# Another order for the first weight pairs of a fused attention and MLP kernel: a table of decode stages in place of whole steps

## The chip, the cores and the metric

The kernel runs on one core of one Trainium2 chip. The metric is the time of one execution on the device, in microseconds (us). The core's engines are named as in the profile: PE is TensorE's matmul (PEld its weight load), DVE is VectorE, ACT is ScalarE, POOL is GpSimd, and SP is SyncE, from whose queue nearly all transfers of this kernel are issued. Each engine runs its own instructions in the order in which they were put there and waits for the others by semaphores.

## The reference, cut to what matters

```python
def reference(q, k, v, n_sink, window, moe_w_in, moe_w_out, moe2_w_in, moe2_w_out):
    x = attention(q, k, v)      # 8 heads of 64, 2 x 768 tokens; a key is seen if it is one of the
                                # first 4 (sinks) or within 128 back
    h = x @ moe_w_in            # 1536 x 512 @ 512 x 2048
    y = (h - tanh(h)) @ moe_w_out
    h = y @ moe2_w_in
    return (h * clip(h + 3, 0, 6) / 6) @ moe2_w_out
```

All four weight matrices come as float64, 32 MB together. The rest is float32.

## The kernel before

**Tokens and groups.** The 1536 tokens are worked through in three chunks of 512. A chunk passes two MLPs, called phase 0 and phase 1. In a phase a hidden layer of 2048 is 16 blocks: h0 to h15 (x times a block of `w_in`, tile `ps_h`) and y0 to y15 (the gated block times a block of `w_out`, added up in four tiles `ps_y`). They run in the order h0, h1, h2, y0, h3, y1, h4, y2 and so on, with y14 and y15 last. One such group is 12 matmuls of 128x512: 4 blocks, three each, since every operand is split into a high and a low part (`mm3`, L178 to L180). Between an h and its y stands the gate: `th` on ACT (L230 in phase 0, L236 in phase 1), its difference or product on DVE (L232, L238), `gh` on ACT (L233, L239), and `gl` on DVE (L234, L240). After y15 the sums are cast to `yh` on ACT (L246, four of them), and phase 1 reads these.

**Weights.** Two groups share a pair of weights, 1 MB of float64. There are 32 pairs, and they are decoded on the chip while chunk 0 runs. The stages of a pair are `w_load` (a transfer on SP into one of 4 raw buffers), `w_scale` (ACT, `dec`, L110), `w_exponent` (DVE, L121), `w_sign` (ACT twice: the low word `r`, L130, and the high word, L132), `w_round` (DVE, L138), `w_keep` (a transfer on SP that stores the decoded pair in DRAM for chunks 1 and 2) and `w_split` (`wh` on ACT, L154, or on POOL for odd pairs from 5 on; `wl` on DVE, L155). There are 4 buffers for `dec`, 2 for `r`, 4 each for `wh` and `wl`. `w_step(p, half)` runs the stages of several pairs at staggered distances: the load of pair p+6, the split of p+1, the low and high word of p+3, and so on.

**Attention.** Chunk 0's attention is 8 heads in pieces (80 in all); its stages are the loads, the casts of k and q (L324, L326), scores on PE (L494), softmax (`sc`, L498 to L503 and L347), transposes of the sink part (`turn_sink`, L525, cast to `pskT` by ACT L529) and of the rest (`turn_p`, L539, copied to `p` by ACT L543), the product with v (`mix`, L588, reading `pskT`, `px` and `vs`), and the cast to the MLP's input (`xh`, L374; `xl` on DVE, L375). Heads 6 and 7 make the last of the four blocks of `xh`, so h0 can run on three blocks before attention has ended. The attention of chunks 1 and 2 is spread over the MLP of the chunk ahead.

**Who sets the order.** `startup` writes attention's pieces of chunk 0 with the first 12 halves of `w_step` among the last 18 of them; `rest` writes the MLP's steps, each with a `w_step`. All of it stands in a block with `schedule_with_timeline_sim=True`: a scheduler decides at build time in what order each engine gets the instructions. `keep_in_program_order` pins an instruction to its place among the others that are pinned.

Of the kernel before, what the change touches and what calls it, by code (L numbers as in the profile page):

```python
# [12 lines left out]
U32 = mybir.dt.uint32  # L13
ACTF = mybir.ActivationFunctionType
# [33 lines left out]
class Mlp:  # L48
# [74 lines left out]
    def w_sign(self, p):  # L123


        if p >= PAIRS:
            return
        raw = self.raw.pop(p)
        r = self.rr[p] = self.r_p.tile([128, 1024], I32, tag="r", name="r")
        self.nc.scalar.activation(out=r, in_=raw[:, :, 0].bitcast(U32), func=ACTF.Copy, scale=2.0 ** -29)  # L130
        upper = r.bitcast(F16).rearrange("p (n two) -> p n two", two=2)[:, :, 1]
        self.nc.scalar.activation(out=upper, in_=raw[:, :, 1].bitcast(F32), func=ACTF.Copy, scale=2.0 ** -100)  # L132

# [137 lines left out]
class Attention:  # L271
# [60 lines left out]
    def split_v(self, it):  # L332
        nc = self.nc
        s = self.st[it]
        s["vs"] = self.v_p.tile([128, len(s["kb"]), 2, 64], F32R, tag="vs", name="vs")
        vh = s["vs"][:, :, 0, :]
        nc.scalar.copy(out=vh, in_=s["vr"])
        nc.gpsimd.tensor_sub(out=s["vs"][:, :, 1, :], in0=s["vr"], in1=vh.bitcast(F32))

    def norm(self, s):  # L340
# [438 lines left out]
def banded(mlp, at):  # L779

    tc = mlp.tc
    with tc.block(schedule_with_timeline_sim=True):
        startup(mlp, at)
        at.wide = False
        rest(mlp, at)


def startup(mlp, at):
    at.sinks()
    first = [p for t in at.ticks(0) for p in t]  # L790
    warm = [(p, h) for p in range(-6, 0) for h in range(2)]
    for n, p in enumerate(first):
        p[0](*p[1:])
        left = len(first) - 1 - n
        while warm and left < 1.5 * len(warm):
            mlp.w_step(*warm.pop(0))


def rest(mlp, at):
# [82 lines left out]
```

## Time and profile before

| | |
|---|---|
| time, median of 3 runs | 682.88 us (680.9 to 683.8) |
| the profiled execution | 682.02 us |
| its span, first to last instruction | 680.3 us |
| PE busy | 635.3 us (93%) |
| DVE busy | 451.8 us (66%) |
| ACT busy | 433.4 us (64%) |
| POOL busy | 154.8 us (23%) |

The profile is of one execution, so sums made from it stand against its own 682.02 us, of which 1.7 us lie outside the span. That execution is 0.86 us under the median of the three runs. The shares are averages over the whole span, while the change touches only its beginning.

### The profile page before, as it was taken

The numbers are of one execution on the slowest core, as the hardware profiler recorded it, in microseconds if no ns is written. First come the engines' busy times: TensorE is split into PE (matmuls) and PEld (weight loads), VectorE is DVE, ScalarE is ACT, GpSimd is POOL, SyncE is SP. The second block draws the span as 40 slices with busy tenths as digits, with TensorE's granted clock in tenths as the row PEclk, the third lists the DMA queues.
The fourth block names the chain that finished last, engine by engine and source line by source line (L and its number), as shares of the span: only waits on it lengthen the run. The fifth ranks groups of instructions, "written<-read, shape, count | busy, mean of one in ns | idle before, by whom it ended". The sixth has DMA issues, their size and how long they took to land.

```text
span 680.3 us, 8590 instructions
## 1 busy us (share of the span) xinstructions
PE 635.3 (93%) x2952; PEld 509.3 (75%) x2952; DVE 451.8 (66%) x824; ACT 433.4 (64%) x742; POOL 154.8 (23%) x198
## 2 busy tenths in 40 slices
PE   1887799995999999999999999999999999999995
PEld 1654688874778778888888788888888888888884
DVE  5996789898799987454665686765454444455431
ACT  3899999999899965444555666655444444354421
POOL 1453011253265654200003344432100000000000
PEclk9997899998899999999999999999999999999998
DMA  5389999987678642233332433122133223221001
GB/s 165 106 275 356 351 377 307 337 303 253 253 239 287 245 168 73 89 123 124 115 120 83 153 112 111 63 87 100 63 124 124 86 101 104 83 69 55 1 0 66
DMA packets 26427, 106.31 MB, mean 156 GB/s; under 512 B 6152, under 2 KB 9224, under 8 KB 18184
## 3 DMA queue, kind: packets, MB, share of 16 engines
q1 hardware_dynamic: 26304, 105.67, 44.8%
q8 instruction: 25, 0.41, 0.2%
q14 instruction: 26, 0.21, 0.1%
q10 hardware_dynamic: 72, 0.02, 0.0%
HBM read 85.76 MB, written 19.92 MB: 155 GB/s over the span
## 4 chain that ended last, share of the span: by engine, by line
PE 66%; ACT 15%; DVE 10%; issue 4%; DMA 3%; POOL 0%; SPq 0%; DVEq 0%; ACTq 0%
PE ps_h L178 10%; PE ps_y L179 10%; PE ps_h L179 10%; PE ps_h L180 10%; PE ps_y L180 10%; PE ps_y L178 10%; ACT r L130 3%; PE ps_a L588 3%; ACT r L132 3%; ACT dec L110 3%; DVE dec L138 2%; DMA raw<-in_w_dram 1%; ACT sc L503 1%; PE ps_a L494 1%; ACT wh L154 1%
## 5 line engine op out<-in xcount | busy, mean ns | idle before, releaser
L179 PE MATMUL ps_y<-gl,wh 128*128 128x512 f32 x384 | 152.2, 396 | 0.5 <-DVE gl L234 0.3
L180 PE MATMUL ps_y<-gh,wl 128*128 128x512 f32 x384 | 151.0, 393 | 0.0
L178 PE MATMUL ps_y<-gh,wh 128*128 128x512 f32 x384 | 133.0, 397 | 7.3 <-ACT gh L233 7.3
L155 DVE TENSOR_TENSOR wl<-raw,wh 128x1024 fp32r<-128x1024 f32 x64 | 79.0, 1235 | 48.4 <-ACT wh L154 46.1
L154 ACT CAST wh<-raw 128x1024 fp32r<-128x1024 f32 x64 | 67.3, 1052 | 48.9 <-PE ps_y L179 36.9
L178 PEld LDWEIGHTS ps_y<-gh,wh 128*128 128x128 f32 x384 | 71.2, 189 | 21.3 <-ACT gh L233 7.5
L179 PEld LDWEIGHTS ps_y<-gl,wh 128*128 128x128 f32 x384 | 72.7, 189 | 17.1 <-DVE gl L234 1.4
L180 PEld LDWEIGHTS ps_y<-gh,wl 128*128 128x128 f32 x384 | 72.8, 189 | 14.9
L178 PE MATMUL ps_h<-xh,wh 128*128 128x512 f32 x192 | 77.0, 403 | 3.6 <-DVE th L232 3.6
L178 PE MATMUL ps_h<-yh,wh 128*128 128x512 f32 x192 | 76.4, 401 | 2.6 <-DVE th L238 2.4
L179 PE MATMUL ps_h<-xl,wh 128*128 128x512 f32 x192 | 76.7, 400 | 0.0
L180 PE MATMUL ps_h<-xh,wl 128*128 128x512 f32 x192 | 76.1, 398 | 0.0
L179 PE MATMUL ps_h<-yl,wh 128*128 128x512 f32 x192 | 76.0, 396 | 0.0
L180 PE MATMUL ps_h<-yh,wl 128*128 128x512 f32 x192 | 76.0, 396 | 0.0
L236 ACT ACTIVATE th<-ps_h,three 128x512 f32<-128x512 f32 x48 | 32.9, 686 | 53.0 <-PE ps_h L180 52.8
L230 ACT ACTIVATE th<-ps_h 128x512 f32<-128x512 f32 x48 | 28.6, 615 | 54.3 <-PE ps_h L180 44.7
L238 DVE SCALAR_TENSOR_TENSOR th<-th,ps_h 128x512 f32<-128x512 f32 x48 | 32.8, 684 | 40.8 <-ACT th L236 40.6
L232 DVE TENSOR_TENSOR th<-ps_h,th 128x512 f32<-128x512 f32 x48 | 32.6, 688 | 30.8 <-ACT th L230 30.6
L503 ACT ACTIVATE sc<-sc,mn 128x132 f32<-128x132 f32 x96 | 38.9, 406 | 14.9 <-DVE mn L499 14.4
L138 DVE CUSTOM_DVE_ANT_0 dec<-dec,r 128x2048 uint16<-128x2048 uint16 x32 | 41.7, 1302 | 9.1 <-ACT r L132 8.9
L178 PEld LDWEIGHTS ps_h<-xh,wh 128*128 128x128 f32 x192 | 36.8, 191 | 12.3 <-DVE th L232 4.0
L234 DVE TENSOR_TENSOR gl<-th,gh 128x512 fp32r<-128x512 f32 x48 | 34.5, 725 | 16.7 <-ACT gh L233 16.4
(105 smaller groups left out, 1150.4 us busy)
## 6 DMA issues: line engine op xcount, KB each, us to landing
raw<-in_w_dram SPq DMA_DIRECT2D x32, 1024.0 KB
raw<-keep SPq DMA_DIRECT2D x32, 1024.0 KB
keep<-dec SPq DMA_DIRECT2D x32, 512.0 KB
raw<-in_qkv_dram SPq DMA_DIRECT2D x8, 810.0 KB
raw<-in_qkv_dram SPq DMA_DIRECT2D x8, 486.0 KB
raw<-in_qkv_dram SPq DMA_DIRECT2D x6, 520.0 KB
out_dram<-ob SPq DMA_DIRECT2D x12, 256.0 KB
raw<-in_qkv_dram SPq DMA_DIRECT2D x8, 324.0 KB
```

The costliest lines, as they stand in the source:

```text
L138: self.nc.vector.tensor_tensor(out=t, in0=t, in1=self.rr.pop(p), op=ALU.add)
L154: nc.scalar.copy(out=wh, in_=src)
L155: nc.vector.tensor_sub(out=wl, in0=src, in1=wh.bitcast(F32))
L178: mm(out=ps, lhsT=wh, rhs=ah, start=first, stop=False)
L179: mm(out=ps, lhsT=wh, rhs=al, start=False, stop=False)
L180: mm(out=ps, lhsT=wl, rhs=ah, start=False, stop=last)
L230: nc.scalar.activation(out=th, in_=ps, func=ACTF.Tanh)
L232: nc.vector.tensor_sub(out=u, in0=ps, in1=th)
L234: self.late.append(lambda: nc.vector.tensor_sub(out=gl, in0=u, in1=gh.bitcast(F32)))
L236: nc.scalar.activation(out=th, in_=ps, func=ACTF.Relu, bias=self.three)
L238: nc.vector.scalar_tensor_tensor(out=u, in0=th, scalar=6.0, in1=ps, op0=ALU.min, op1=ALU.mult)
L503: nc.scalar.activation(out=s["sc"][:, i, :], in_=s["sc"][:, i, :], func=ACTF.Exp, scale=-1.0, bias=s["mn"][:, i:i + 1], accum_out=s["sm"][ ...
```

## The change

The 12 halves of `w_step` in `startup` are replaced by a table. Each row gives a number of attention pieces still to come, a stage and a pair; the stage is written when so many are left. Altogether the same stages of the same pairs are written ahead of `rest` as before. Two pins are added: the low-word pass (L130) of pairs 0 to 3, and the cast of v (L337) of chunk 1's heads 0 to 2.

```diff
@@ w_sign
-        self.nc.scalar.activation(out=r, in_=raw[:, :, 0].bitcast(U32), func=ACTF.Copy, scale=2.0 ** -29)
+        ins = self.nc.scalar.activation(out=r, in_=raw[:, :, 0].bitcast(U32), func=ACTF.Copy, scale=2.0 ** -29)
+        if p < 4:
+            self.tc.keep_in_program_order(ins)
@@ split_v
-        nc.scalar.copy(out=vh, in_=s["vr"])
+        ins = nc.scalar.copy(out=vh, in_=s["vr"])
+        if it[0] == 1 and it[1] < 3:
+            self.tc.keep_in_program_order(ins)
@@ startup
+WARM = (
+    (52, "load", 0), (48, "load", 1), (44, "load", 2), (40, "load", 3),
+    (36, "scale", 0), (33, "exponent", 0), (31, "sign", 0), (27, "round", 0),
...
+    (0, "exponent", 3), (0, "scale", 4),
+)
...
-    warm = [(p, h) for p in range(-6, 0) for h in range(2)]
+    warm = list(WARM)
     for n, p in enumerate(first):
         p[0](*p[1:])
-        left = len(first) - 1 - n
-        while warm and left < 1.5 * len(warm):
-            mlp.w_step(*warm.pop(0))
+        while warm and len(first) - 1 - n <= warm[0][0]:
+            _, stage, pair = warm.pop(0)
+            getattr(mlp, f"w_{stage}")(pair)
```

The line numbers of the changed kernel lie 2 higher from L132 on and 4 higher from L338 on (L134 is the high word, L156 `wh`, L180 to L182 the three matmuls, L232 `th`, L235 `gh`, L248 `yh`, L378 `xh`, L529 the sink's transpose, L533 `pskT`, L547 `p`).

**Place one, the end of attention, ACT.** Before, the last two casts `xh` stand among decode passes of several pairs (raw64_662 is pair 2, raw64_752 pair 5; 719 is pair 4, wh_787 and wh_845 are those of pairs 1 and 2):

```order
L374 CAST xh_131<-ps_a_736 64x512
L337 CAST vs_1249<-raw_1046 128x5x64
L529 CAST pskT_750<-ps_a_745 8x512
L110 ACTIVATE dec_774<-raw64_719 128x1024
L154 CAST wh_787<-dec_671 128x1024
L130 ACTIVATE r_818<-raw64_685 128x1024
L154 CAST wh_845<-dec_700 128x1024
L130 ACTIVATE r_872<-raw64_719 128x1024
L132 ACTIVATE r_818<-raw64_685 128x1024
L374 CAST xh_131<-ps_a_776 64x512
```

Now, from the cast `xh` of head 6 to the first gate (raw64_420 is pair 2, raw64_454 pair 3; the last cast `xh` is the one of head 7):

```order
L378 CAST xh_131<-ps_a_737 64x512
L339 CAST vs_1249<-raw_1046 128x5x64
L547 COPY p_758<-ps_a_753 128x512
L156 CAST wh_787<-dec_590 128x1024
L533 CAST pskT_751<-ps_a_746 8x512
L378 CAST xh_131<-ps_a_763 64x512
L110 ACTIVATE dec_774<-raw64_420 128x1024
L130 ACTIVATE r_777<-raw64_420 128x1024
L232 ACTIVATE th_806<-ps_h_793 128x512
L130 ACTIVATE r_818<-raw64_454 128x1024
L232 ACTIVATE th_838<-ps_h_823 128x512
```

Between the last two casts `xh` six decode passes stood and one stands now; pair 2 begins only behind attention. Counted over ACT's whole order, nine decode passes that stood ahead of the last cast `xh` stand behind it now: three `dec`, three low words, two high words and one `wh`.

**Place one, PE.** The transpose of head 7's sink part (now L529, ahead of `pskT`) stood in front of the MLP's first matmul before; now it stands behind 16 of them, and its `mix` behind 11 more. The rows are those around the transpose (ps_h_823 is h1, ps_h_851 is h2):

```order
L180 MATMUL ps_h_823<-xh_131,wh_608 128x512
L529 MATMUL ps_a_746<-ident_r_188,psk_734 8x128 x4
L181 MATMUL ps_h_823<-xl_132,wh_608 128x512
L182 MATMUL ps_h_823<-xh_131,wl_609 128x512
L180 MATMUL ps_h_851<-xh_131,wh_787 128x512
```

**Place two, the end of phase 0, ACT.** Before, the rows from `th` of h15 (th_1626) on (raw64_1663 and raw64_1762 belong to the same two pairs as dec_1808 and dec_1898):

```order
L230 ACTIVATE th_1626<-ps_h_1613 128x512
L326 ACTIVATE qh_1875<-raw_1671 128x512
L324 CAST k_1877<-raw_1671 128x660
L474 CAST vsk_1660<-vkr_1494 8x2x64
L132 ACTIVATE r_2080<-raw64_1762 128x1024
L110 ACTIVATE dec_1808<-raw64_1663 128x1024
L503 ACTIVATE sc_1570,sm_1572<-sc_1570,mn_1571 128x132
L337 CAST vs_1657<-raw_1491 128x5x64
L360 COPY ready1_70<-ps_a_1677 64x512
L503 ACTIVATE sc_1570,sm_1572<-sc_1570,mn_1571 128x132
L110 ACTIVATE dec_1898<-raw64_1762 128x1024
L529 CAST pskT_1747<-ps_a_1742 8x512
```

The next row was gh_1627, the gate of h15. Now:

```order
L232 ACTIVATE th_1626<-ps_h_1613 128x512
L134 ACTIVATE r_1805<-raw64_1537 128x1024
L130 ACTIVATE r_1895<-raw64_1605 128x1024
L235 CAST gh_1559<-th_1558 128x512
L328 ACTIVATE qh_1875<-raw_1671 128x512
L326 CAST k_1877<-raw_1671 128x660
L507 ACTIVATE sc_1570,sm_1572<-sc_1570,mn_1571 128x132
L235 CAST gh_1627<-th_1626 128x512
```

Behind the last gate, up to `yh`, stand rows that stood ahead of it. Ahead of the last `gh` of phase 0 ACT now has two `dec`, two low words, three high words, one `wh` and five small casts fewer. The four casts `yh` stood together; now a high word stands between the second and the third and a low word between the third and the fourth.

**Place three, SP.** Before, chunk 0's loads (raw_475 and raw_545 are q, k and v of heads 6 and 7; vkr is v at the sinks) came first, then the first pair (raw64_606):

```order
L459 DMA vkr_1278<-in_vs_dram 8x64 x2
L459 DMA vkr_1494<-in_vs_dram 8x64 x2
L267 DMA raw_405<-in_qkv_dram 128x4x260
L459 DMA vkr_1674<-in_vs_dram 8x64 x2
L267 DMA raw_475<-in_qkv_dram 128x4x260
L267 DMA raw_545<-in_qkv_dram 128x4x260
L94 DMA raw64_606<-in_w64_dram 128x2048
```

Now the four first pairs (raw64_363 to raw64_454) stand among them:

```order
L94 DMA raw64_363<-in_w64_dram 128x2048
L94 DMA raw64_392<-in_w64_dram 128x2048
L463 DMA vkr_1278<-in_vs_dram 8x64 x2
L463 DMA vkr_1494<-in_vs_dram 8x64 x2
L269 DMA raw_409<-in_qkv_dram 128x4x260
L94 DMA raw64_420<-in_w64_dram 128x2048
L94 DMA raw64_454<-in_w64_dram 128x2048
L269 DMA raw_485<-in_qkv_dram 128x4x260
```

So the first two pairs are ahead of the small loads `vkr` and of head 5's load, and the next two ahead of head 6's.

## Rows read from the trace of the kernel before

**Rows 1.** The page: the chain that ended last, by engine.

```profile
PE 66%; ACT 15%; DVE 10%; issue 4%; DMA 3%; POOL 0%; SPq 0%; DVEq 0%; ACTq 0%
```

**Rows 2.** Windows: stretch, length, busy us by engine (instructions), granted clock, DMA share, GB/s.

```profile
17.00:51.00 34.00, 29.22 (x166) 20.31 (x166) 31.63 (x121) 30.69 (x96) 16.59 (x29) 1.00 0.60 190
...
45.00:157.00 112.00, 103.41 (x457) 80.17 (x455) 96.12 (x151) 111.90 (x157) 29.95 (x30) 0.95 0.92 330
...
180.00:240.00 60.00, 59.25 (x302) 47.92 (x300) 57.48 (x101) 56.58 (x99) 31.64 (x32) 1.00 0.72 252
240.00:260.00 20.00, 18.30 (x96) 15.00 (x95) 17.30 (x34) 13.39 (x29) 13.11 (x16) 1.00 0.46 163
260.00:600.00 340.00, 339.26 (x1578) 275.64 (x1577) 196.01 (x328) 172.99 (x302) 55.87 (x78) 1.00 0.29 99
```

**Rows 3.** The wait of PE at the first gate: total, times, longest.

```profile
PE ps_h L178 <- DVE th L232: 3.6, 1, 3.6
```

**Rows 4.** Timeline of ACT at attention's end: start, duration, what.

```profile
58.69 0.57 ACT L543 COPY p<-ps_a 128x512 f32<-128x512 f32 x1
...
61.42 1.13 ACT L110 ACTIVATE dec<-raw 128x1024 f32<-128x1024 f32 x1
62.46 1.37 ACT L132 ACTIVATE r<-raw 128x1024 f16<-128x1024 f32 x1
63.70 0.56 ACT L374 CAST xh<-ps_a 64x512 fp32r<-64x512 f32 x1
...
66.04 1.03 ACT L154 CAST wh<-dec 128x1024 fp32r<-128x1024 f32 x1
66.97 1.15 ACT L130 ACTIVATE r<-raw 128x1024 int32<-128x1024 uint32 x1
68.03 1.03 ACT L154 CAST wh<-dec 128x1024 fp32r<-128x1024 f32 x1
...
71.39 0.58 ACT L374 CAST xh<-ps_a 64x512 fp32r<-64x512 f32 x1
...
81.74 1.17 ACT L233 CAST gh<-th 128x512 fp32r<-128x512 f32 x2
```

**Rows 5.** Timeline of PE at attention's end.

```profile
61.14 0.73 PE L178 MATMUL ps_h<-xh,wh 128*128 128x512 f32 x1
...
65.86 0.67 PE L588 MATMUL ps_a<-pskT,yh 8*64 8x512 f32 x2
...
68.12 0.50 PE L178 MATMUL ps_h<-xh,wh 128*128 128x512 f32 x1
68.45 0.39 PE L179 MATMUL ps_h<-xl,wh 128*128 128x512 f32 x1
68.68 0.40 PE L180 MATMUL ps_h<-xh,wl 128*128 128x512 f32 x1
...
80.11 0.63 PE L180 MATMUL ps_h<-xh,wl 128*128 128x512 f32 x1
80.54 0.63 PE L178 MATMUL ps_h<-xh,wh 128*128 128x512 f32 x1
```

**Rows 6.** Timeline of ACT at the end of phase 0.

```profile
168.50 0.61 ACT L233 CAST gh<-th 128x512 fp32r<-128x512 f32 x1
...
174.00 1.98 ACT L246 CAST yh<-ps_y 128x512 fp32r<-128x512 f32 x4
...
180.69 0.69 ACT L236 ACTIVATE th<-ps_h,three 128x512 f32<-128x512 f32 x1 [0.49 <-PE ps_h L180]
```

**Rows 7.** Timeline of PE: y15 (in brackets the idle time ahead of it).

```profile
169.16 2.08 PE L178 MATMUL ps_y<-gh,wh 128*128 128x512 f32 x4 [7.31 <-ACT gh L233]
```

**Rows 8.** Timeline of ACT, then of PE, at phase 1's first gate.

```profile
184.35 0.62 ACT L239 ACTIVATE gh<-th 128x512 fp32r<-128x512 f32 x1
...
186.36 1.14 PE L178 MATMUL ps_y<-gh,wh 128*128 128x512 f32 x4
```

**Rows 9.** The chain of waits, 30 to 40 us: start, length, what.

```profile
32.41 5.58 DMA raw<-in_w_dram
```

More of the change, by code (lines that the diff above doesn't have):

```diff
@@ L785, in banded @@
         rest(mlp, at)
+WARM = (
+    (52, "load", 0), (48, "load", 1), (44, "load", 2), (40, "load", 3),
+    (36, "scale", 0), (33, "exponent", 0), (31, "sign", 0), (27, "round", 0),
+    (24, "load", 4), (22, "scale", 1), (21, "keep", 0), (20, "split", 0), (18, "exponent", 1),
+    (13, "sign", 1), (8, "round", 1), (7, "keep", 1),
+    (0, "load", 5), (0, "scale", 2), (0, "exponent", 2), (0, "sign", 2), (0, "scale", 3),
+    (0, "exponent", 3), (0, "scale", 4),
+)
 def startup(mlp, at):
```

## Prediction

> **What bounds the kernel now.** I read the chain of waits first. PE has 66% of it, ACT 15%, DVE 10% [rows 1]: PE bounds the kernel for most of the time, but not always. The windows say when. From 260 to 600 us PE is busy for 339.26 of 340 us, so nothing that happens there can be gained by another order of the weights' decoding [rows 2]. From 45 to 157 us ACT is busy for 111.90 of 112 us, at 96 of 112 on DVE and 103 of 112 on PE: the decode passes and gates on ACT set the pace [rows 2]. From 17 to 51 us, while attention runs with little decoding, no engine is quite full, but DVE has only 2.4 and ACT only 3.3 of 34 us idle [rows 2]. The list of PE's waits and the timeline give PE's large holes in the ACT stretch: 3.6 us for the first gate's `th` [rows 3] and 7.31 us ahead of y15, for `gh` [rows 7]. After 180 us it is idle for 0.75 of 60 and then 1.70 of 20 us [rows 2]. So the order matters through one thing: when ACT gets to the gates, and how much PE then waits until about 260 us. The kernel's time is its own 682.02 us plus or minus what PE loses or gains until there.
>
> **What the change does, part by part.** Nothing is added to or taken from the work. What ACT pays for a pair is read from start to start: `dec` 1.04, high word 1.24, `wh` 0.93, low word 1.06, in all 4.27 us [rows 4]; a cast of 128x512 costs 0.5 (four in 1.98) [rows 6], and I take 0.4 to 0.5 for the other small ones, as an estimate from it.
>
> *Earlier passes.* Pair 0 and most of pair 1 now lie among heads 4 to 6. Up to the copy `p` of head 7, ACT's order holds two `dec`, two low words, two high words and one `wh`, 7.6 us; before it held three, two, one and one, 7.4 us. So this piece can't come sooner by it. Two small casts (`xh` of head 6, `vs`) have moved ahead of it as well, 0.9 us, and that `xh` needs PE's `mix` of head 6, for which I reckon with 1.5 us of waiting. `p` stood at 58.69 [rows 4]; now 58.7 + 0.2 + 0.9 + 1.5 = 61.3. Bounds: 59.8 without the wait; later by 2 if the decode passes, earlier now, push DVE's softmax, which has nearly no room [rows 2].
>
> *Attention's tail.* From here the order on PE decides. Behind `p`'s transposes come 16 MLP matmuls. One takes 0.23 us (68.45 to 68.68) [rows 5], 16 take 3.7; then head 7's sink transpose (0.4, the estimate for a small cast), 11 more matmuls (2.6, with ACT's `pskT` beside them), and `mix`, 2.3 us (65.86 to 68.12) [rows 5]. If PE has done `p`'s transposes at 60.7, that's 64.4, 64.8, 67.4 and 69.7, so the last `xh` comes some 1.7 us ahead of its 71.39 [rows 4]. But the nine passes that were moved behind it are 3 x 1.04 + 3 x 1.06 + 2 x 1.24 + 0.93 = 9.7 us. ACT did them before without idling [rows 2]; now it has one `wh` and one `pskT` in 8 us. **ACT is therefore 9.7 - 1.7 = 8.0 us behind, at equal work.** That's the term on which the rest hangs. It would be 0 if ACT were never to wait here.
>
> *First gates.* Ahead of `gh` of h0 ACT now has two `dec`, three low words, three high words, three `wh` and a `vs` fewer, 12.1 us. It stood at 81.74 [rows 4]; now 81.7 + 8.0 - 12.1 = 77.6. PE has then done h0 to h2 and waits for y0, since y0 now stands fourth; it will have waited about 5 us from some 73 on, instead of 3.6 [rows 3]. After the 3.6 us the clock was at the lower of its two levels, 1.2 GHz: matmuls 0.43 us apart (80.11 to 80.54) instead of 0.23 [rows 5]. I expect the same few slow matmuls after the new hole, so no difference from that.
>
> *The end of phase 0.* Ahead of the last `gh` ACT has two `dec`, two low, three high words, one `wh` and five small casts fewer: 2.1 + 2.1 + 3.7 + 0.9 + 1.9 = 10.7. It stood at 168.50 [rows 6]; now 168.5 + 8.0 - 10.7 = 165.8, and y15 at about 166.5 instead of 169.16 [rows 7]. The 7.31 us hole shrinks; what remains lies ahead of y14, since between the last two `gh` only three small casts stand now.
>
> *yh gives it back.* The rows that left the stretch ahead of the gate now stand between it and `yh`: 0.5 for the gate, a `wh`, a high and a low word, two `dec` and six small casts, 8.2 us. So the first `yh` starts at 174.0, exactly as before [rows 6]. Before, the four were done by 176.0; now a high and a low word stand among them and the last ends at 178.3. PE's first block of phase 1 needs all four. Then `dec`, high, low, `sc`, high, `sc` (5.4): the first gate of phase 1 at 183.6, against 180.69 [rows 6]: 2.9 us later, with one high and one low word (2.3 us) still owed. A little further on the two orders hold the same work.
>
> *What PE makes of it.* A gate of phase 1 ends at 184.97 and its y starts at 186.36 [rows 8], so 1.4 of the 2.9 us is slack; 1.5 is lost. The owed passes cost up to 2.3 more. Against that, PE's idle time from 180 to 260 us, 0.75 + 1.70 = 2.5 [rows 2], is there to be used up: I take 1.5 + 2.3 - 2.5 = **+1.3 us**. Both ends: 0 if the owed passes fall into ACT's idle time of 240 to 260 us (13.39 busy of 20) [rows 2], +3.8 if nothing is got back.
>
> *Transfers.* The pairs' loads are 1 MB each. One took 5.58 us from issue to landing beside other traffic [rows 9]. Two now stand ahead of head 5's load and `vkr`. From 17 to 51 us the DMA engines are busy for a share of 0.60 [rows 2], so there is room; the loads' earlier landing gains nothing either, since ACT wasn't waiting for them (0.10 us idle in 112) [rows 2]. I take 0; bounds -1 and +5.6, one whole load. The Trainium skill ("DMA: Bandwidth & Descriptors", section "Queues, rings and completion order") says that each of the DMA engines takes the descriptors of a ring in the order of issue; by that the two loads would stand in full ahead of head 5's. No row here shows one load held up by another; it is the reason for the upper bound's rival below.
>
> *The pins* issue nothing and are costed with the order that results; the one on `vs` concerns a cast of half a microsecond in a stretch in which it is neither first nor last, so 0.
>
> **Sum:** 682.02 + 1.3 = 683.3 us, 0.4 over the median of the runs shown, while 0.5% (3.4 us) is about the least that a measurement of this kernel can tell from no change.
>
> **The rivals.**
>
> *Not measurable (my forecast), 0.50.* The hole ahead of y15 closes partly, and `yh` and attention's tail take it back. 680 to 686.4.
>
> *Faster, 0.27.* ACT's idle time at the tail is shorter than I walked it. For it: `p`'s wait of 1.5 us and the 16 matmuls ahead of the sink's transpose are read from an order, not from a time; and before, PE's work of head 7 was stretched by ACT's queue. If 5 of the 8.0 us go, the first gate of phase 1 stands at 178.6, 2.1 ahead of 180.69; the owed 2.3 fall away in ACT's idle time, and the matmuls of y15 after the 7.31 us hole, four in 2.08 us where a warm y takes 1.14 [rows 7, 8], run at 0.23 instead of 0.43: 12 x 0.2 = 2.4. That is 682.0 - 2.1 - 2.4 = 677.5. It decides at about 4 us of ACT idle time or less between `p` and the last `xh`. Against it: PE's order is fixed, and the 27 matmuls and the `mix` alone take 8.6 us at the full clock.
>
> *Slower, 0.23.* The tail's MLP matmuls run at the lower level. A hole of 3.6 us did bring the lower level further on [rows 3, 5], and in the tail PE now waits for `p`, for softmax and for `mix`'s operands between short stretches of work. 27 matmuls x 0.20 = 5.4 us more ahead of the last `mix`, while ACT waits; carried on in lockstep: 683.3 + 5.4 = 688.7, or 686.5 if only half of them are slow. It decides if more than ten of the 27 are 0.43 apart. The Trainium skill speaks for this rival: "TensorE: Matmul & The Clock Gate", section "HAM oscillation — how this bites in real kernels", has short bursts of matmuls between waits each begin at half rate, so that the price is paid with every wait, and this change adds waits at the tail. The slow matmuls after the 3.6 us hole agree with it. The first MLP matmuls before (61.14 on) soon ran 0.23 apart [rows 5], which is why I don't make it the likeliest. Held-up loads (head 5 later by up to 5.6 us) would end at the same place, at about 687.
>
> **The numbers.** Forecast 683.3. The range reaches from 677.5, the faster case's value, to 688.0, most of the slower case's: about 2 in 10 lie outside. Faster by over 0.5% 0.27, within 0.50, slower 0.23.
>
> **What would show it.** Right: `xh` of head 7 near 70 us with some 7 us of ACT idle time in the 9 us ahead of it, ended by PE; PE's hole ahead of y0 of some 5 us; y15 near 166 to 167; `yh` from 174 on, spread over 4 us; the first gate of phase 1 near 183; PE without holes from 260 on. The faster case: `xh` of head 7 before 67 and `yh` before 171. The slower one: matmuls 0.43 apart between 60 and 70 us and `xh` after 73. Wrong altogether: PE idle after 260 us, or a wait for a load in PE's or ACT's list.

## The result and the profile after

The changed kernel takes 688.68 us (median of 6 runs, 687.64 to 690.16), the kernel before 683.16 in its runs beside it (680.66 to 684.22). The ratio is 1.0093, 95% interval 1.0075 to 1.0111: it is **slower, by 5.5 us** between the medians. 683.3 was forecast, with 0.23 for slower; the measured time lies just above the range.

The profiled execution has a span of 687.7 us, 7.4 more than that of before. The page, busy time by engine and then the chain that ended last:

```profile
PE 640.5 (93%) x2952; PEld 512.8 (75%) x2952; DVE 454.3 (66%) x824; ACT 433.2 (63%) x742; POOL 156.9 (23%) x198
...
PE 71%; DVE 10%; ACT 10%; DMA 4%; issue 3%; POOL 1%; SPq 0%; DVEq 0%; ACTq 0%; POOLq 0%
```

PE ran the same 2952 matmuls, and was busy for 640.5 instead of 635.3 us with them: 5.2 of the 7.4 us are matmuls that took longer, and 2.2 are idle time (687.7 - 640.5 against 680.3 - 635.3). ACT's share of the chain has fallen from 15% to 10%, PE's has risen. The stretches that answer to [rows 2] (stretch, length, busy us by engine, granted clock, DMA share, GB/s):

```profile
17.00:51.00 34.00, 24.99 (x126) 17.82 (x126) 29.22 (x103) 29.95 (x86) 11.54 (x23) 0.90 0.72 250
45.00:157.00 112.00, 98.97 (x420) 74.97 (x419) 87.94 (x144) 99.46 (x151) 24.74 (x25) 0.91 0.80 273
240.00:260.00 20.00, 18.82 (x98) 15.47 (x96) 18.73 (x37) 14.35 (x32) 12.56 (x14) 1.00 0.74 272
260.00:600.00 340.00, 339.26 (x1588) 275.85 (x1588) 197.41 (x332) 172.30 (x304) 61.86 (x84) 1.00 0.30 102
...
46.00:48.20 2.20, 2.16 (x11) 1.50 (x9) 0.60 (x3) 2.15 (x9) 0.00 (x0) 0.55 0.73 183
...
51.00:60.00 9.00, 8.77 (x34) 5.54 (x35) 8.09 (x20) 6.39 (x15) 3.29 (x6) 0.62 0.65 200
60.00:70.00 10.00, 8.71 (x47) 6.06 (x46) 5.07 (x10) 5.34 (x13) 5.88 (x8) 1.00 0.79 261
```

From 45 to 157 us ACT, which was idle for 0.1 us before, is now idle for 12.5. From 260 us on PE is as full as before, so all of it was lost ahead of that. From 17 to 51 us the granted clock (a mean of its two levels, 2.4 GHz counting as 1.00 and 1.2 GHz as 0.50), at 1.00 before, is 0.90, and from 51 to 60 us it is 0.62 although PE is busy for 8.77 of 9 us.

ACT at attention's end, which answers to [rows 4]: start, duration, what, and in brackets the idle time ahead and what ended it.

```profile
52.24 0.59 ACT L547 COPY p<-ps_a 128x512 f32<-128x512 f32 x1 [0.75 <-PE ps_a L543]
...
55.10 0.40 ACT L507 ACTIVATE sc<-sc,mn 128x132 f32<-128x132 f32 x1 [0.84 <-DVE mn L503]
...
57.33 0.58 ACT L378 CAST xh<-ps_a 64x512 fp32r<-64x512 f32 x1 [0.49 <-PE ps_a L592]
58.44 0.58 ACT L533 CAST pskT<-ps_a 8x512 fp32r<-8x512 f32 x1 [0.54 <-PE ps_a L529]
...
61.44 0.58 ACT L378 CAST xh<-ps_a 64x512 fp32r<-64x512 f32 x1 [0.38 <-PE ps_a L592]
...
65.40 0.58 ACT L378 CAST xh<-ps_a 64x512 fp32r<-64x512 f32 x1 [2.02 <-PE ps_a L592]
...
66.24 0.58 ACT L547 COPY p<-ps_a 128x512 f32<-128x512 f32 x1
66.72 1.05 ACT L156 CAST wh<-dec 128x1024 fp32r<-128x1024 f32 x1
70.00 0.58 ACT L533 CAST pskT<-ps_a 8x512 fp32r<-8x512 f32 x1 [2.23 <-PE ps_a L529]
74.83 0.58 ACT L378 CAST xh<-ps_a 64x512 fp32r<-64x512 f32 x1 [4.25 <-PE ps_a L592]
...
82.69 0.64 ACT L235 CAST gh<-th 128x512 fp32r<-128x512 f32 x1
```

From 66.24 on this is the forecast's tail: one `wh` and one `pskT` between `p` and the last `xh`, and 6.5 us of waiting for PE. But `p` itself is 7.55 us later than at 58.69, where 2.6 was forecast. And the end of phase 0, which answers to [rows 6]:

```profile
170.78 0.61 ACT L235 CAST gh<-th 128x512 fp32r<-128x512 f32 x1
...
179.20 1.04 ACT L248 CAST yh<-ps_y 128x512 fp32r<-128x512 f32 x2
...
182.94 0.56 ACT L248 CAST yh<-ps_y 128x512 fp32r<-128x512 f32 x1
...
188.73 0.66 ACT L238 ACTIVATE th<-ps_h,three 128x512 f32<-128x512 f32 x1
```

PE, for [rows 5, 7]: a hole of 2.55 us in attention and behind it a slow `mix` (2.73 us for its eight matmuls with `px`), then a hole of 3.07 and a slower `mix` (3.25; 1.73 where the clock is up again). Then come the MLP's matmuls 0.23 apart, and the hole ahead of y0 with y0's first four matmuls in 2.08.

```profile
42.74 0.30 PE L498 MATMUL ps_a<-k,qh 128*128 128x132 f32 x1 [2.55 <-DVE mn L503]
...
43.98 2.73 PE L592 MATMUL ps_a<-px,vs 128*64 128x256 f32 x8
...
51.23 0.97 PE L543 MATMUL ps_a<-ident,sc 128*128 128x128 f32 x4 [3.07 <-DVE sc L351]
...
54.04 3.25 PE L592 MATMUL ps_a<-px,vs 128*64 128x256 f32 x8
...
59.67 1.73 PE L592 MATMUL ps_a<-px,vs 128*64 128x256 f32 x8
...
66.02 0.40 PE L181 MATMUL ps_h<-xl,wh 128*128 128x512 f32 x1
66.25 0.40 PE L182 MATMUL ps_h<-xh,wl 128*128 128x512 f32 x1
...
83.39 2.08 PE L180 MATMUL ps_y<-gh,wh 128*128 128x512 f32 x4 [5.55 <-ACT gh L235]
```

### The profile page after: what moved, and what is told of

The parts are those of the page before. It is cut to its first block, busy times and chain, and to the rows that moved or that the text cites. A ratio compares the mean times of both kernels' runs of the same rounds, so it can differ in the third digit from the quotient of the medians.

```text
span 687.7 us, 8568 instructions
## 1 busy us (share of the span) xinstructions
PE 640.5 (93%) x2952; PEld 512.8 (75%) x2952; DVE 454.3 (66%) x824; ACT 433.2 (63%) x742; POOL 156.9 (23%) x198
## 4 chain that ended last, share of the span: by engine, by line
PE 71%; DVE 10%; ACT 10%; DMA 4%; issue 3%; POOL 1%; SPq 0%; DVEq 0%; ACTq 0%; POOLq 0%
PE ps_h L180 11%; PE ps_h L181 10%; PE ps_h L182 10%; PE ps_y L181 10%; PE ps_y L182 10%; PE ps_y L180 10%; PE ps_a L592 5%; DMA keep<-dec 2%; PE ps_a L498 2%; ACT dec L110 2%; ACT r L134 2%; DVE dec L140 2%; ACT r L130 2%; DVE wl L157 1%; DMA vkr<-in_vs_dram 1%
## 5 line engine op out<-in xcount | busy, mean ns | idle before, releaser
L182 PE MATMUL ps_y<-gh,wl 128*128 128x512 f32 x384 | 151.0, 395 | 0.0
L180 PE MATMUL ps_y<-gh,wh 128*128 128x512 f32 x384 | 132.1, 398 | 7.4 <-ACT gh L235 5.9
L156 ACT CAST wh<-raw 128x1024 fp32r<-128x1024 f32 x64 | 67.3, 1052 | 49.2 <-PE ps_y L181 36.9
L180 PEld LDWEIGHTS ps_y<-gh,wh 128*128 128x128 f32 x384 | 71.3, 189 | 22.7 <-ACT gh L235 6.5
L182 PEld LDWEIGHTS ps_y<-gh,wl 128*128 128x128 f32 x384 | 72.8, 190 | 14.9
L180 PE MATMUL ps_h<-yh,wh 128*128 128x512 f32 x192 | 76.8, 404 | 2.8 <-ACT yh L248 2.1
L180 PE MATMUL ps_h<-xh,wh 128*128 128x512 f32 x192 | 76.5, 400 | 0.7 <-ACT xh L378 0.7
L182 PE MATMUL ps_h<-yh,wl 128*128 128x512 f32 x192 | 76.5, 398 | 0.0
L182 PE MATMUL ps_h<-xh,wl 128*128 128x512 f32 x192 | 76.4, 398 | 0.0
L232 ACT ACTIVATE th<-ps_h 128x512 f32<-128x512 f32 x48 | 28.6, 601 | 53.6 <-PE ps_h L182 44.7
L498 PE MATMUL ps_a<-k,qh 128*128 128x264 f32 (+1 forms) x96 | 30.1, 328 | 16.7 <-DVE k L327 12.0
L180 PEld LDWEIGHTS ps_h<-yh,wh 128*128 128x128 f32 x192 | 36.4, 189 | 12.0 <-ACT yh L248 2.5
```

What stands on the lines that cost most here:

```text
L156: nc.scalar.copy(out=wh, in_=src)
L180: mm(out=ps, lhsT=wh, rhs=ah, start=first, stop=False)
L182: mm(out=ps, lhsT=wl, rhs=ah, start=False, stop=last)
L498: nc.tensor.matmul(out=ps[:, 0:w], lhsT=s[nm][:, 128 * i:128 * (i + 1)], rhs=rhs, start=(n == 0), stop=(n == 1))
```

## The experiments

All kernels here compute the whole reference. To take the table apart, the steps of the kernel before were written as such a table too; with it, and without the new pins, the scheduler gives every engine the same order as before, instruction by instruction:

```python
OLD = ((17, "load", 0), (14, "load", 1), (13, "scale", 0), (11, "load", 2), (11, "exponent", 0), (10, "scale", 1),
       (8, "load", 3), (8, "exponent", 1), (7, "sign", 0), (7, "scale", 2), (5, "load", 4), (5, "round", 0),
       (5, "exponent", 2), (4, "keep", 0), (4, "sign", 1), (4, "scale", 3), (2, "load", 5), (2, "split", 0),
       (2, "round", 1), (2, "exponent", 3), (1, "keep", 1), (1, "sign", 2), (1, "scale", 4))
```

Each kernel was measured beside the kernel before, in 4 to 10 runs. The table gives the median time and the ratio to the kernel before with its 95% interval. The other columns are of one execution each, the profiled one: its time, ACT's idle time between 17 and 90 us (73 less its busy time in that window), when `p` and `xh` of head 7 start, and when the `th` of phase 1's first gate starts.

| kernel | median us | ratio | profiled one us | ACT idle 17 to 90 | p of head 7 | last xh | phase 1's first gate |
|---|---|---|---|---|---|---|---|
| before | 681.7 to 683.2 | 1 | 682.02 | 3.4 | 58.69 | 71.39 | 180.69 |
| a_loads | 680.11 | 0.9971 (0.9955 to 0.9986) | 679.44 | 5.1 | 63.02 | 75.44 | 179.08 |
| b_late | 679.67 | 0.9955 (0.9935 to 0.9974) | 680.47 | 6.9 | 59.19 | 65.81 | 182.79 |
| ab_pins | 681.46 | 0.9993 (0.9973 to 1.0014) | 680.81 | 7.5 | 59.62 | 66.32 | 180.42 |
| vsk_b | 680.92 | 0.9985 (0.9964 to 1.0006) | 676.97 | 2.9 | 55.04 | 60.85 | 179.11 |
| d_pins | 683.64 | 1.0023 (0.9990 to 1.0057) | 688.25 | 6.2 | 57.65 | 67.08 | 181.73 |
| b_late_nopins | 684.01 | 1.0037 (1.0020 to 1.0054) | 684.13 | 5.3 | 57.69 | 68.44 | 182.06 |
| c_nopins | 684.23 | 1.0034 (1.0019 to 1.0050) | 682.61 | 7.3 | 68.62 | 82.30 | 183.45 |
| d_nopins | 688.09 | 1.0101 (1.0065 to 1.0137) | 685.35 | 13.9 | 66.50 | 77.69 | 189.20 |
| **the change** | 688.68 | 1.0093 (1.0075 to 1.0111) | 689.43 | 15.6 | 66.24 | 74.83 | 188.73 |
| p0_only | 690.03 | 1.0115 (1.0087 to 1.0143) | 689.36 | 13.7 | 60.90 | 72.85 | 189.51 |
| c_early | 691.73 | 1.0133 (1.0107 to 1.0159) | 691.95 | 16.8 | 70.04 | 79.31 | 190.52 |
| warm_after | 692.86 | 1.0138 (1.0104 to 1.0172) | 694.72 | 15.3 | 62.27 | 74.42 | 192.67 |
| f_tail | 693.64 | 1.0168 (1.0140 to 1.0197) | 693.52 | 14.0 | 65.78 | 72.82 | 189.97 |

**a_loads: the early loads alone.** The kernel before with

```diff
-(17, "load", 0), (14, "load", 1), (11, "load", 2), (8, "load", 3)
+(52, "load", 0), (48, "load", 1), (44, "load", 2), (40, "load", 3)
```

> The kernel before with only the loads of pairs 0 to 3 at the changed table's places (52, 48, 44, 40 pieces left), every other stage where it was, no new pins. In the changed kernel the copy p of head 7 started at 66.24 us instead of 58.69 and everything behind it was late by the same amount. Theory 'loads' (the early megabytes hold up vkr and the loads of heads 5 and 6): p of head 7 at 61 or later, time 2 to 5 us over the kernel before. Theory 'passes' (the decode passes of pairs 0 and 1 on ACT and DVE, put among heads 3 to 5, hold up attention and PE's clock falls): p of head 7 within 1 us of 58.7 and the time within 2 us of before.

`p` of head 7 came at 63.02, as the theory of the loads has it, and yet the time fell by 2 us. Neither theory expected the two together. Attention ran later with the loads early, and the time doesn't show it; ACT had passes to do meanwhile and was idle for 5.1 us from 17 to 90. So when `p` comes doesn't tell the time; that was the first hint at what does.

**c_early: only pairs 0 and 1 early.** The changed kernel with

```diff
-(0, "scale", 2), (0, "exponent", 2), (0, "sign", 2), (0, "scale", 3), (0, "exponent", 3)
+(7, "scale", 2), (5, "exponent", 2), (4, "scale", 3), (2, "exponent", 3), (1, "sign", 2)
```

and load 5 and scale 4 likewise at 2 and 1.

> The changed kernel with the stages of pairs 2 to 4 put back to their old places among the last heads; loads, pairs 0 and 1 and the pins as changed. Theory 'passes': p of head 7 at 65 to 67 as in the changed kernel, time 686 to 690. Theory 'tail' (what costs is that pairs 2 to 4 were moved behind attention, so that ACT idles for some 8 us): ACT's idle time ahead of the last xh falls under 4 us and the time to 682 to 685.

691.73 us: with the pins the early passes are slow without the late part, and ACT's idle time didn't fall under 4 us ahead of the last `xh`. With the pins the theory of the tail alone is out. The same table without them (c_nopins, below) takes 684.23, so c_early doesn't price the early passes by themselves.

**b_late: only pairs 2 to 4 late.** The changed table with the loads and all stages of pairs 0 and 1 at their places in OLD.

> The changed kernel with the loads and the stages of pairs 0 and 1 put back to their old places; pairs 2 to 4 behind attention's last piece and the pins as changed. Theory 'passes': p of head 7 at 56 to 59, time 680 to 684. Theory 'tail': ACT idles ahead of the last xh as in the changed kernel and the time is 685 to 689.

679.67, under the kernel before by 0.45%: with the pins the late part, by which I had explained ACT's falling behind, costs nothing when pairs 0 and 1 are left where they were. ACT was idle for 6.9 us from 17 to 90. Without the pins it does cost (b_late_nopins, below).

**d_pins: the pins alone**, on OLD.

> The kernel before with the two new pins alone and the old order of stages. Theories 'passes', 'loads' and 'tail' all expect no difference: within 2 us of before. If the pins themselves cost, the time is 3 us or more over before.

683.64, interval 0.9990 to 1.0057: no difference that shows. But its ten runs spread from 680.6 to 688.5, and the profiled one took 688.25.

**p0_only: pair 0 early, pair 1 at its old places**, pairs 2 to 4 late, pins as changed. Load 4 and the keep of pair 1 are back at 5 and 1 as well.

```diff
-(48, "load", 1), (44, "load", 2), (40, "load", 3), (22, "scale", 1), (18, "exponent", 1), (13, "sign", 1), (8, "round", 1)
+(14, "load", 1), (11, "load", 2), (10, "scale", 1), (8, "load", 3), (8, "exponent", 1), (4, "sign", 1), (2, "round", 1)
```

> The changed kernel with the loads 1 to 3 and the stages of pair 1 put back to their old places: only pair 0 is decoded early. With pairs 0 and 1 early and pairs 2 to 4 late (the changed kernel) the median was 688.7, with none early and pairs 2 to 4 late 679.7. If each pair that is put among the heads costs its share: 683 to 686, p of head 7 at 61 to 64 us. If the cost lies in pair 1 alone (its passes fall on heads 5 to 7): 679 to 681. If in pair 0 alone: 687 to 689.

690.03, over all three expectations: with the pins and the late part, pair 0 alone is enough. Its `p` of head 7 comes at 60.90, 5.3 us ahead of the changed kernel's, with no gain: ACT idles for 13.7 us. From b_late it differs by where one pair is loaded and decoded, 4.3 us of ACT's work.

**ab_pins: early loads and late pairs**, the two parts that were faster.

> The two parts of the change that were faster alone, together: loads 0 to 3 early, every decode pass of pairs 0 and 1 at its old place, pairs 2 to 4 behind attention's last piece, the pins as changed. Loads alone gave 680.1, the late pairs alone 679.7 against 682.2 for the kernel before. If they gain at different places: 676 to 678. If both gain the same time at the end of phase 0 or of attention: 679 to 681. If the order that the scheduler builds decides more than either part: anything up to 684.

681.46. The gains don't add; only the last of the three expectations, that the scheduler's order decides, holds the value, and it excludes little.

**f_tail: another order on PE at attention's end.** The changed kernel with

```diff
+    sink, mix = at.sink_ins, at.mix_ins          # head 7's last sink transpose, last mix matmul
...
-            mlp.step(GROUPS * c + i)
+            if c == 0 and i in (0, 1, 2):
+                with at.tc.issue_after((sink, sink, mix)[i].ins):
+                    mlp.step(GROUPS * c + i)
+            else:
+                mlp.step(GROUPS * c + i)
```

> The changed kernel with another order on PE alone at attention's end: head 7's sink transpose ahead of the MLP's first matmul instead of behind 16, its mix ahead of h2 instead of behind 11 matmuls of it. Theory 'tail' (ACT's 2.2 and 4.3 us of waiting there are on the path): the last xh starts 2.5 to 4 us earlier against the copy p of head 7 and the time is 684 to 687. If ACT's waiting at the tail is not on the path: 688 to 690. Theory 'passes' expects p of head 7 unchanged near 66.

From `p` to the last `xh` it took 7.0 instead of 8.6 us, a smaller gain than was expected, and the time rose to 693.64, over both expectations. PE now waits elsewhere (4.8 us for a `wh` further on). This order of PE at the tail doesn't mend the kernel; others were not tried.

**warm_after: two more matmuls ahead of each score.** They do work that nobody reads:

```diff
+        if self.wide:
+            for _ in range(2):
+                nc.tensor.matmul(
+                    out=ps[:, 264:512], lhsT=s["qh"][:, 128 * i:128 * (i + 1)],
+                    rhs=s["k"][:, 0:2, :].rearrange("p a c -> p (a c)")[:, 0:248],
+                    start=True, stop=True, skip_group_check=True,
+                )
```

> The changed kernel with two more matmuls of 248 columns ahead of each score of chunk 0, into columns of the bank that nobody reads: 64 matmuls, some 7 us more work for PE while it has 10 us idle in attention. Theory 'clock' (the early passes open holes on PE, its clock falls, and attention's own matmuls then take about 4 us longer): the granted clock from 34 to 60 us rises from 0.89 and 0.62 to over 0.95, p of head 7 comes at 62 to 64 instead of 66.2. Theory 'work' (ACT's and DVE's passes themselves hold attention up): p of head 7 at 66 or later, and 0 to 7 us more in all. The scheduler also orders the later gates a little differently here, so attention's end tells more than the time.

The window from 34 to 60 us, of this kernel and then of the changed one:

```profile
34.00:60.00 26.00, 22.19 (x144) 15.72 (x144) 24.47 (x76) 25.85 (x67) 11.34 (x16) 1.00 0.54 175
```

```profile
34.00:60.00 26.00, 19.93 (x93) 13.08 (x93) 22.55 (x69) 22.14 (x53) 7.06 (x15) 0.80 0.58 176
```

The granted clock rose from 0.80 to 1.00 and `p` of head 7 came at 62.27, 4.0 us earlier than in the changed kernel, with more work on PE. Not all of that is the clock's: the order on ACT differs too. In the changed kernel `xh` of head 6, its wait of 2.02 us and a `vs` stand ahead of `p`; here they stand behind it. The cast `pskT` of head 6 is the last piece ahead of which both have the same work (but for one `sc` more here): it came at 60.31 instead of 62.41, 2.1 us earlier. It had been behind before: at the first `xh` this kernel is 2.5 us later (31.20 against 28.69), with a granted clock of 0.80 from 17 to 34 us against 0.91. So between these two pieces attention took 4.6 us less here. Of the 4.9 us by which `p` missed the forecast, 2 to 4.6 go with the lower clock by this pair of runs, which settles it no closer. And the time didn't follow: it was 692.86. ACT still ran out of work, and its waits for the two last `xh` were 5.18 and 4.02 us, since the scheduler put most of head 6's `mix` behind 15 MLP matmuls here, the first eight 0.43 apart. An earlier `p` came with more of ACT's idle time behind it.

**c_nopins and d_nopins: the twins.** c_nopins is c_early without the two pins, d_nopins the changed kernel without them. The two have one difference, the places of pairs 2 to 4 (and of load 5): 7 to 1 pieces ahead of attention's end in c_nopins, behind it in d_nopins.

> Loads and pairs 0 and 1 early as in the changed kernel, pairs 2 to 4 at their old places, and no new pins, so that the scheduler may put passes of later pairs where ACT waits; ACT's order holds some 15 us more of decode passes ahead of the last xh than in the changed kernel. With the pins the same table gave 691.7. Theory 'filler' (early passes cost nothing by themselves; what costs is ACT idling among the last heads with no pass left to do): ACT idle from 17 to 90 us falls from 16.8 us to under 8 and the time is 680 to 685. Theory 'passes' (decode passes among heads 3 to 5 hold attention up for good): ACT idle falls too, but the time stays at 686 to 692, since the first gate comes as late.

> The changed kernel without the two new pins: the table alone. ACT's order holds 4.5 us more of decode passes ahead of the last xh than with the pins. Theory 'filler': ACT idle from 17 to 90 us falls from 15.6 to about 11 us and the time to 684 to 687. If the pins play no part: 687 to 690.

Both run alike until about 60 us. Then ACT, first of c_nopins (the last `xh` at 82.30) and then of d_nopins (at 77.69):

```profile
64.69 3.21 ACT L110 ACTIVATE dec<-raw 128x1024 f32<-128x1024 f32 x3
...
69.10 2.16 ACT L130 ACTIVATE r<-raw 128x1024 int32<-128x1024 uint32 x2
71.17 1.03 ACT L154 CAST wh<-dec 128x1024 fp32r<-128x1024 f32 x1
72.10 2.60 ACT L132 ACTIVATE r<-raw 128x1024 f16<-128x1024 f32 x2
74.57 0.56 ACT L374 CAST xh<-ps_a 64x512 fp32r<-64x512 f32 x1
...
82.30 0.58 ACT L374 CAST xh<-ps_a 64x512 fp32r<-64x512 f32 x1
```

```profile
72.02 0.58 ACT L374 CAST xh<-ps_a 64x512 fp32r<-64x512 f32 x1 [1.68 <-PE ps_a L588]
72.50 0.46 ACT L337 CAST vs<-raw 128x320 fp32r<-128x320 f32 x1
72.86 0.57 ACT L529 CAST pskT<-ps_a 8x512 fp32r<-8x512 f32 x1
77.69 0.58 ACT L374 CAST xh<-ps_a 64x512 fp32r<-64x512 f32 x1 [4.26 <-PE ps_a L588]
```

And their windows from 17 to 90 us, c_nopins first:

```profile
17.00:90.00 73.00, 56.07 (x255) 37.08 (x256) 56.74 (x148) 65.68 (x137) 22.41 (x38) 0.93 0.74 265
```

```profile
17.00:90.00 73.00, 53.35 (x244) 35.48 (x244) 51.84 (x146) 59.06 (x132) 20.67 (x38) 0.91 0.64 223
```

c_nopins ends attention 4.6 us later and is 3.9 us faster between the medians (2.7 between the two profiled executions). Its ACT has decode passes between the pieces and does 6.6 us more work by 90 us (65.68 against 59.06). This is the filler theory's forecast (under 8 us idle, 680 to 685: measured 7.3 and 684.2). For d_nopins it expected 11 us idle and 684 to 687: measured 13.9 and 688.1, so there it missed; in the whole change the pins play no part that shows. In c_early they do: with them ACT's order there leaves 16.8 us idle instead of 7.3, and the time is 7.5 us higher.

**vsk_b and b_late_nopins.** b_late with one pin more (the cast `vsk` of chunk 1's heads 0 to 3 queued behind what is written ahead of it), and b_late without the pins.

> The kernel with the late pairs alone (b_late, 679.7) with one pin more: the cast vsk of chunk 1's heads 0 to 3 is queued behind what is written ahead of it. In all kernels so far ACT waits there at 21 to 28 us for the load vkr of a chunk 1 head, 1.2 to 2.2 us. If this wait is on the path: 676 to 678.5. If attention's other engines set the pace there: 679 to 681.

> The late pairs alone without the new pins. With them: 679.7, ACT idle from 17 to 90 us 6.9 us. Theory 'filler': ACT's idle time is as small or smaller, time 677 to 682. If the pins are what makes b_late faster than the kernel before: 682 to 684.

680.92 and 684.01. The pin on `vsk` takes ACT's wait for the load at 21 to 28 us away (no wait for a load is left there), ends attention 5 us earlier than b_late, and the median doesn't show it. But its runs reach from 676.97 to 684.62, and the profiled one, which has the last `xh` at 60.85, is the quickest of them; whether the others end attention as early isn't shown. Without the two pins b_late is slower than the kernel before by 0.37%: its gain hangs on the pins. Here the filler theory missed: ACT idles less than in b_late, 5.3 us, but the time is over the 682 that it allowed. No version beats the kernel before by more than b_late: 0.45% by the ratio, 2.5 us between the medians.

## Why the prediction was wrong, point by point

**The step that failed is the first one, the earlier passes, by the size of one term: ACT's waiting ahead of `p` of head 7.** I reckoned with 1.5 us of it, at the `xh` of head 6, and with none before. The windows of the two executions up to that copy, before and after:

```profile
17.00:58.69 41.69, 32.79 (x179) 22.25 (x180) 36.46 (x128) 38.33 (x108) 20.30 (x34) 0.96 0.67 223
```

```profile
17.00:66.24 49.24, 38.70 (x186) 26.42 (x187) 40.70 (x130) 40.15 (x109) 17.61 (x34) 0.86 0.72 246
```

ACT's work up to there grew by 1.8 us (1.1 forecast), its idle time from 3.4 to 9.1, by 5.7 instead of 1.5. The wait at head 6's `xh` was 2.02; five more, of 0.4 to 0.8 us each and 3.0 together, lie between 51 and 62 us, four of them for PE. The granted clock fell from 0.96 to 0.86. The bound that I gave (up to 2 us more) was too narrow: it counted DVE's passes, and not that PE would then run attention itself at the lower clock. By warm_after 2 to 4.6 us of `p`'s lateness go with that clock. What the rest goes with isn't shown.

**Every later step held, shifted by that.** Forecast and measured: last `xh` 69.7 and 74.83; first `gh` 77.6 and 82.69; last `gh` 165.8 and 170.78; first `yh` 174.0 and 179.20; last `yh` ended 178.3 and 183.50; first gate of phase 1 183.6 and 188.73. All are late by 5.0 to 5.2 us, so the distances between them were right to 0.2 us: the tail's waiting, the passes owed, `yh` that gives back what the hole ahead of y15 gave.

**What is got back later.** The first gate of phase 1 is 8.0 us later than before (188.73 against 180.69 in [rows 6]), the span 7.4 us longer. I had counted 2.9 of lateness as 1.3 in the end, 1.6 got back; only 0.6 us was. So of the 6.1 us by which the profiled execution misses the forecast 5.1 stand at this gate already (4.2 of them the waiting ahead of `p`, 0.7 ACT's work there), and 1.0 come behind it. I had counted PE's 2.5 us of idle time from 180 to 260 us as used up. In the same stage, 8 us later, PE is idle for 3.3 us (56.74 us busy of 60 from 188 to 248, 20.00 of 20 from 248 to 268).

**The loads** were priced at 0, with bounds of -1 and +5.6. In a_loads the time is 2.1 us lower with them, outside those bounds, and `p` comes 4.3 us later, which was not forecast.

**The pins** were priced at 0. For the whole change that holds (688.68 with them, 688.09 without). For its parts it doesn't: they add 7.5 us to the early part (c_early, c_nopins) and take 4.3 from the late part (b_late, b_late_nopins).

**The rivals.** The slower one gave 688.7 by its full price, which is the measured time, but by luck, not for its reason: it put the lower clock on the 27 MLP matmuls at the tail. These ran 0.23 apart (66.02 to 66.25), at a granted clock of 1.00 from 60 to 70 us. The slow stretch lay ahead of it, in attention from 34 to 60 us. The mechanism that it borrowed from the Trainium skill ("TensorE: Matmul & The Clock Gate", section "HAM oscillation — how this bites in real kernels"), bursts between waits that start at half rate, agrees with the 3.07 us hole and the `mix` of 3.25 us behind it, in another place than I put it. But the clock was down ahead of that hole already, 0.55 from 46.0 to 48.2 us; and behind the hole of 2.55 us PE began at 1.00 (42 to 44 us) and only then fell (0.64 from 44 to 46). The faster rival's condition, little waiting between `p` and the last `xh`, didn't come about.

**What the runs put in place of it.** The forecast treated ACT's lateness at the tail as the price of moving pairs 2 to 4. The runs give neither part of the table a price of its own. Without the pins all four combinations are there: the late part alone costs 2.3 us (b_late_nopins, 684.01), the early part with its loads alone 2.5 (c_nopins, 684.23), both 6.4 (d_nopins, 688.09; the kernel before took 681.74 beside all three). With the pins the late part alone takes 679.67 (b_late), the early one alone 691.73 (c_early), both 688.68, neither 683.64 (d_pins). So what a part costs depends on the order that the scheduler builds around it.

What the quicker and the slower kernels differ in is ACT's idle time. Eight kernels, the kernel before among them, with 7.5 us or less of it from 17 to 90 us have medians of 679.7 to 684.2, and six with 13.7 or more 688.1 to 693.6. Within a group it doesn't order them. The step between is the start of phase 1: its first gate comes at 179.1 to 183.5 us in the profiled executions of the eight and at 188.7 to 192.7 in those of the six. What follows varies by as much again, 494 to 505 us from that gate to the end of the span, so single executions of the two groups overlap: d_pins's took 688.25 with 6.2 us idle, d_nopins's 685.35 with 13.9.

Why the passes are missed is shown by the twins, with the early passes in both: ACT runs out of work when the passes that could stand behind its waits are gone. In the changed kernel seven of its casts and copies between 50 and 75 us wait for PE, 10.7 us in all; in the kernel before decode passes stand between them. What stays open: why early loads alone put `p` 4 us later, why the pins turn the price of either part, and what makes the stretch behind phase 1's first gate longer or shorter; f_tail and warm_after are the slowest with no more idle time than the changed kernel.

## What to carry to other kernels

Work that an engine can do at any time is worth most where that engine would wait. Before it is moved ahead into a stretch with little room, look at what was queued behind the waits that it leaves. Count the idle time of the engine that sets the pace over the whole stretch, not when one piece arrives: c_nopins ended attention 4.6 us later than its twin and was 3.9 us faster. Try the parts of a change in every combination: the late part alone came out 2.5 us under the kernel before with the pins and 2.3 us over it without them. And a walk along rows gives distances well (0.2 us over some 115 us here), but where several engines are nearly full a guess for "some waiting" also has to carry the slower clock that came with the waits here.

## What was not expected of the hardware

From 51 to 60 us the granted clock was 0.62 while PE was busy for 8.77 of 9 us; before, it was 0.73 in the same stretch with PE busy for 4.89 of 9:

```profile
51.00:60.00 9.00, 4.89 (x16) 2.65 (x17) 6.02 (x9) 8.95 (x15) 4.38 (x7) 0.73 0.98 369
```

So a busy PE in the profile was not a PE at the upper clock here. With 64 useless matmuls strewn over attention (warm_after) PE ran at 1.00 from 34 to 60 us. Head 6's `pskT` came 2.1 us earlier than in the changed kernel; the whole kernel came out slower all the same.
